# A decode layer of attention and MLP on one core: 64 KB rows in three slots, exp from PSUM, columns made on TensorE

## Chip, cores, metric

One core of one Trainium2 chip. The metric is the device time of one execution in microseconds (us), as the median of several runs. Each ratio compares a kernel with runs of the kernel before on the same chip.

## The reference, cut

One token, x of 1024 channels. The result is x + attention(LN x) + MLP-mixer(LN x). Attention reads a cache of 4 key heads of 65536 keys of 128 channels, each shared by 8 query heads:

```python
q = (xn @ wq)                                   # 1024 x 4096
scores = einsum("bhqd,bhkd->bhqk", q, k) * 128 ** -0.5
p = softmax(scores);  o = einsum("bhqk,bhkd->bhqd", p, v)
attn = o.reshape(B, 1, 4096) @ wo               # 4096 x 1024
# mixer: four groups of channels are shifted along the tokens, zeros move in
h = gelu(layernorm(x) @ w1);  hs = concat(shift(h, +1, -1, +2, -2)) @ w2
x1 = x + hs
out = x1 + gelu(layernorm(x1) @ w3) @ w4        # 1024 x 3584 x 1024
```

With one token, each shift leaves only zeros, so hs is zero whatever w1 and w2 are. K and V are 67.1 MB each, all weights together 35.7 MB: 169.87 MB in all.

## The kernel before

A list of loads is worked through in order. Loads go to five slots of 32 KB per partition (and one of 16 KB for w1, w2, wo); a load is issued as soon as its slot has been consumed. A unit is 16384 keys of one key head.

```python
BIG_BUFS = 5; UKEYS = 16384; SUBS = 2; SETS = 4
stream = [("wq",0), ("wq",1), ("w3",0), ("w3",1), ("w1",0), ("K",0), ("K",1), ("V",0)]
for u in range(2, NU):
    stream += [("K", u), ("V", u - 1)]            # K one unit ahead of V
    ...                                           # w2 and three wo in between
stream += [("wo", HKV - 1), ("V", NU - 1), ("w4", 0), ("w4", 1)]

def done(self, it):                               # called after the last reader of a tile
    self.tiles.pop(it); self.held[...] -= 1; self.pump()
...
            src = cache[0, g, b * UKEYS:(b + 1) * UKEYS, :].rearrange("(p ct) d -> p (ct d)", p=P)
            nc.sync.dma_start(out=t[:], in_=src)  # 128 rows of 32 KB
```

Keys lie in the rows with the channel inside, but the score products sum over partitions, so VectorE transposes K in place in blocks of 32 x 32 words. TensorE multiplies it with copies of the queries. Then the softmax of the unit and the product with V:

```python
    nc.vector.transpose(out=words, in_=words)                       # L372, 128 x 2048 words
    nc.tensor.matmul(sc[:, sub, :], lhsT=qdiag[:, c0:c0 + P], ...)  # L383, 32 per unit
    nc.vector.tensor_scalar(out=s_sb[:], in0=sc[:], scalar1=SCALE, ..., op1=ALU.max,
                            accum_out=mx[:])                        # L390, copy to SBUF with the maximum
    ...                                                             # maximum over partitions: L400 to L419
    nc.scalar.activation(out=p_sb[:], in_=s_sb, func=ACTF.Exp, bias=nball[:, b:b + 1], ...)   # L421
    nc.vector.transpose(out=pT, in_=p_sb)                           # L424
    nc.tensor.matmul(oacc[32 * q:32 * (q + 1), :], lhsT=pT[...], rhs=vt[...],
                     tile_position=(0, 32 * q))                     # L457, 32 per unit, four columns of tiles
```

A small clock of ticks spreads the softmax steps of unit u between the score products of unit u+1. At the end w4 comes in six pieces (8, 8, 8, 2, 1, 1 of its 28 columns), and its products wait for each piece. The h of the MLP goes to DRAM and back to become columns; x is loaded once as a row and once as 128 slivers of 16 bytes.

## Time and profile before

| | before |
|---|---|
| median | 405.87 us (405.79 to 405.95) |
| profiled span | 404.1 us |
| moved by the load queue | 169.87 MB in 6912 packets |
| DMA share and rate, 60 to 360 us | 1.00, 429 to 431 GB/s |
| busy PE, DVE, ACT | 58%, 52%, 8% |
| last 24 products of w4 | start at 397.63 us |

The DMA share is how much of the time the 16 DMA engines are busy on average. It is 1.00 over 300 us, so the DMA is the bound there. The packet count is worth a check against the code: the loads have 128 rows each, so 8 per DMA engine; 48 loads make 384 rows per engine, plus one completion per load and engine, 432, and 432 x 16 = 6912.

### The profile page before, as it was taken

The numbers are of one execution on the slowest core, as the hardware profiler recorded it, in microseconds if no ns is written. First come the engines' busy times: TensorE is split into PE (matmuls) and PEld (weight loads), VectorE is DVE, ScalarE is ACT, GpSimd is POOL, SyncE is SP. The second block draws the span as 40 slices with busy tenths as digits, with TensorE's granted clock in tenths as the row PEclk, the third lists the DMA queues.
The fourth block names the chain that finished last, engine by engine and source line by source line (L and its number), as shares of the span: only waits on it lengthen the run. The fifth ranks groups of instructions, "written<-read, shape, count | busy, mean of one in ns | idle before, by whom it ended". The sixth has DMA issues, their size and how long they took to land.

```text
span 404.1 us, 3287 instructions
## 1 busy us (share of the span) xinstructions
PE 236.2 (58%) x1392; PEld 94.1 (23%) x1392; DVE 211.8 (52%) x241; ACT 34.3 (8%) x61; POOL 6.4 (2%) x19
## 2 busy tenths in 40 slices
PE   0382727839483859292929394565658561948094
PEld 0131202313131323031313231122213220313041
DVE  0310046957658584566585473738393934665310
ACT  1000210110101011001010101010101010010100
POOL 4000100000000000000000000000000000000000
PEclk9998558688897979797978979596959895879769
DMA  8999999999999999999999999999999999999993
GB/s 357 422 415 431 449 416 439 440 418 429 448 417 425 454 409 430 444 431 417 448 428 418 436 420 438 428 444 423 428 436 428 422 436 435 431 426 430 420 427 144
DMA packets 7237, 170.11 MB, mean 421 GB/s; under 512 B 1070, under 2 KB 1074, under 8 KB 1462
## 3 DMA queue, kind: packets, MB, share of 16 engines
q1 hardware_dynamic: 6912, 169.87, 98.1%
q8 instruction: 11, 0.18, 0.2%
q0 software_dynamic: 160, 0.02, 0.0%
q10 hardware_dynamic: 150, 0.01, 0.0%
q14 instruction: 4, 0.03, 0.0%
HBM read 169.88 MB, written 0.01 MB: 420 GB/s over the span
## 4 chain that ended last, share of the span: by engine, by line
DMA 49%; PE 30%; DVE 10%; another core or an unknown queue 6%; ACT 2%; issue 2%; SPq 0%; DVEq 0%; ACTq 0%
DMA big<-in_A_k_cache_dram 35%; PE sc L383 21%; DMA big<-in_B_w_dram 11%; DVE big L372 5%; PE oacc L457 4%; DMA x_bf<-in_A_x_dram 3%; DVE s_sb L390 2%; PE psq L250 1%; ACT p_sb L421 1%; PE psB L179 1%; PE psB L239 1%; DVE pT L424 1%; PE pm_mx L400 1%; DVE og L439 0%
## 5 line engine op out<-in xcount | busy, mean ns | idle before, releaser
L383 PE MATMUL sc<-big,qdiag 128*128 128x512 bf16 x512 | 150.0, 461 | 104.9 <-DVE big L372 104.9
L372 DVE STREAM_TRANSPOSE big<-big 128x2048 f32<-128x2048 f32 x64 | 142.4, 2279 | 49.4 <-DMA big<-in_A_k_cache_dram 49.4
L383 PEld LDWEIGHTS <-qdiag 128*128 128x128 bf16 x512 | 56.8, 111 | 193.2 <-issue 100.3
L457 PE MATMUL oacc<-big,pT 128*32 128x512 bf16 x512 | 37.7, 396 | 9.7 <-DMA big<-in_A_v_cache_dram 9.7
L390 DVE TENSOR_SCALAR_CACHE_REDUCE s_sb<-sc 128x1024 f32<-128x1024 f32 x16 | 19.6, 1225 | 45.0 <-PE sc L383 45.0
L424 DVE STREAM_TRANSPOSE pT<-p_sb 128x1024 bf16<-128x1024 bf16 x16 | 19.8, 1240 | 16.8 <-ACT p_sb L421 16.8
L463 ACT COPY ob<-oacc 128x512 f32<-128x512 f32 x12 | 7.0, 586 | 214.6 <-PE oacc L457 214.6
L421 ACT ACTIVATE p_sb<-s_sb,nball 128x1024 bf16<-128x1024 f32 x16 | 18.4, 1150 | 76.5 <-DVE nball L419 76.5
L457 PEld LDWEIGHTS <-pT 128*32 128x32 bf16 x512 | 14.0, 99 | 28.7 <-issue 17.1
L400 PE MATMUL pm_mx<-ident_f,mx 128*1 128x128 f32 x16 | 4.3, 270 | 16.7 <-DVE s_sb L390 16.7
L419 DVE COPY nball<-pm_mx 128x1 f32<-128x1 f32 x16 | 2.5, 153 | 17.5 <-PE pm_mx L413 17.5
L250 PE MATMUL psh<-big,ln_rep_b 128*32 128x512 bf16 x56 | 5.5, 505 | 8.8 <-DMA big<-in_B_w_dram 8.8
L466 DVE SCALAR_TENSOR_TENSOR og<-oacc,wb,og 128x512 f32<-128x512 f32 x4 | 3.0, 751 | 12.5 <-PE oacc L457 12.5
L179 PE MATMUL psB<-big,cols_h 128*1 128x512 bf16 x56 | 7.7, 420 | 1.6 <-DMA big<-in_B_w_dram 1.6
L189 PE MATMUL pm_ln<-ln_rowsum_a,ones_f 128*128 128x1 f32 x2 | 0.6, 348 | 13.7 <-DVE sel L213 13.7
L179 PE MATMUL psB<-w,oT 128*1 128x512 bf16 x64 | 7.6, 379 | 0.0
L473 PE MATMUL pm_e<-og,selbig 128*128 128x128 f32 x32 | 5.6, 326 | 3.2 <-DVE nball L419 2.3
L402 DVE TENSOR_REDUCE negm<-pm_mx 1x8 f32<-1x128 f32 x16 | 4.4, 275 | 5.4 <-PE pm_mx L400 5.4
L250 PEld LDWEIGHTS <-ln_rep_b 128*32 128x32 bf16 x72 | 3.4, 120 | 15.0 <-issue 12.2
L183 DVE CAST xT<-x_bf 128x8 f32<-128x8 bf16 x1 | 0.2, 172 | 12.0 <-DMA x_bf<-in_A_x_dram 12.0
L400 PEld LDWEIGHTS pm_mx<-ident_f,mx 128*1 128x1 f32 x16 | 1.3, 79 | 21.9 <-DVE s_sb L390 21.9
L439 DVE SCALAR_TENSOR_TENSOR og<-ob,wb,og 128x512 f32<-128x512 f32 x8 | 6.0, 751 | 0.1
(98 smaller groups left out, 80.5 us busy)
## 6 DMA issues: line engine op xcount, KB each, us to landing
big<-in_A_k_cache_dram SPq DMA_DIRECT2D x16, 4096.0 KB, 46.1
big<-in_A_v_cache_dram SPq DMA_DIRECT2D x16, 4096.0 KB, 39.9
big<-in_A_wq_dram SPq DMA_DIRECT2D x2, 4096.0 KB, 16.9
w<-in_A_wo_dram SPq DMA_DIRECT2D x4, 2048.0 KB, 30.1
big<-in_B_w_dram SPq DMA_DIRECT2D x2, 3584.0 KB, 34.3
big<-in_B_w_dram SPq DMA_DIRECT2D x3, 2048.0 KB, 40.7
w<-in_B_w_dram SPq DMA_DIRECT2D x2, 2048.0 KB, 42.6
big<-in_B_w_dram SPq DMA_DIRECT2D x1, 512.0 KB, 43.4
```

Source lines behind the costliest of these rows:

```text
L179: nc.tensor.matmul(psB[32 * j:32 * j + 1, :], lhsT=lhsT, rhs=rhs, start=False, stop=False, tile_position=(0, 32 * j), skip_group_check=True)
L250: nc.tensor.matmul(acc[i][32 * q:32 * q + 32], lhsT=rep[:, c, :], rhs=wt[:, k, 512 * s:512 * (s + 1)], start=first, stop=last, tile_positi ...
L372: nc.vector.transpose(out=words, in_=words)
L383: nc.tensor.matmul(sc[:, sub, :], lhsT=qdiag[:, c0:c0 + P], rhs=cols[:, sub, s, :, b, :, r], start=(s == 0 and b == 0 and r == 0), stop=(s ...
L390: nc.vector.tensor_scalar(out=s_sb[:], in0=sc[:], scalar1=SCALE, scalar2=None, op0=ALU.mult, op1=ALU.max, accum_out=mx[:])
L400: nc.tensor.transpose(pm[0:1, 0:P], unit.pop((u, "mx"))[:, 0:1], ident_f[:])
L421: nc.scalar.activation(out=p_sb[:], in_=unit.pop((u, "ssb"))[:], func=ACTF.Exp, bias=nball[:, b:b + 1], scale=1.0, accum_out=group[(g, "la ...
L424: nc.vector.transpose(out=pT[:].rearrange("p u n -> p (u n)"), in_=p_sb[:].rearrange("p u n -> p (u n)"))
L439: nc.vector.scalar_tensor_tensor(out=og[:], in0=ob[:], scalar=wb[:, k:k + 1], in1=og[:], op0=ALU.mult, op1=ALU.add)
L457: nc.tensor.matmul(oacc[32 * q:32 * (q + 1), :], lhsT=pT[:, sub, 32 * t:32 * (t + 1)], rhs=vt[:, sub, :, t, :], start=(sub == 0 and t < 4) ...
L463: nc.scalar.copy(out=ob[:], in_=oacc[:])
L473: nc.tensor.matmul(pe[:, 0:P], lhsT=selbig[:, cg, :], rhs=og[:, 128 * cg:128 * (cg + 1)], start=(cg == 0), stop=(cg == 3))
```

## The change

Its intent: fewer and larger loads, fewer instructions, no trips through DRAM. Three parts:

1. All large loads go into three slots of 64 KB rows; a unit is 32768 keys, the score tile has four banks, and the pipelining by ticks goes.
2. The maximum and exp read the score tile in PSUM; the copy in SBUF goes.
3. x, h and the zero vector become columns by small TensorE products; w3 is read with a stride so that the columns come out in w4's order.

```diff
-UKEYS = 16384
-SUBS = 2
+ROW = 32768
+SUBS = 4
 SETS = 4
-BIG_BUFS = 5
-W4_PIECES = ((8, 8), (8, 2, 1, 1))
+SLOTS = 3
+W4_PIECES = (16, 8, 2, 1, 1)
 ...
+    stream = ["wq", "w3", "w12"]
+    for u in range(NU):
+        if u == NU - 1:
+            stream += [("K", u), "wo", ("V", u)]
+        else:
+            stream += [("K", u), ("V", u)]
+    stream.append("w4")
 ...
-    x_bf = const.tile([P, DC], BF16, name="x_bf")
-    nc.scalar.dma_start(out=x_bf[:], in_=A_x[0, 0, :].rearrange("(p c) -> p c", c=DC))
 ...
+    for c in range(DC):
+        nc.tensor.matmul(px[:, c:c + 1], lhsT=x_row[0:1, c::DC], rhs=pick4[0:1, 0:1], start=True, stop=True)
 ...
+        wt = st.tiles["w3"][:, 0:DC * F].rearrange("p (c m k) -> p c k m", c=DC, k=FC)
 ...
+        for ik in range(8):
+            nc.tensor.matmul(ph[:, ik, :], lhsT=h_rows[:, ik // 4, P * (ik % 4):P * (ik % 4 + 1)], rhs=pick4[:],
+                             start=True, stop=True)
 ...
-        s_sb = spool.tile([P, SUBS, 512], F32, name="s_sb", tag="s_sb")
-        nc.vector.tensor_scalar(out=s_sb[:], in0=sc[:], scalar1=SCALE, scalar2=None, op0=ALU.mult, op1=ALU.max,
-                                accum_out=mx[:])
+        nc.vector.reduce_max(out=mx[:], in_=sc[:].rearrange("p e n -> p (e n)"), axis=AX.X)
 ...
+        nc.scalar.activation(out=p_sb[:], in_=sc[:], func=ACTF.Exp, bias=nball[:, b:b + 1], scale=SCALE,
+                             accum_out=group["lall"][:, b:b + 1])
 ...
+    for u in range(NU - 1):
+        compute_k(u)
+        compute_v(u)
+    compute_k(NU - 1)
+    for g in range(HKV - 1):
+        project(g)
+    compute_v(NU - 1)
+    project(HKV - 1)
+    st.done("wo")
+    compute_w4(0, FC)
```

## The prediction

> **What bounds the kernel now.** I read the page first: slices, then the chain.
>
> ```profile
> span 404.1 us, 3287 instructions
> ...
> PE 236.2 (58%) x1392; PEld 94.1 (23%) x1392; DVE 211.8 (52%) x241; ACT 34.3 (8%) x61; POOL 6.4 (2%) x19
> ...
> DMA  8999999999999999999999999999999999999993
> ...
> q1 hardware_dynamic: 6912, 169.87, 98.1%
> ...
> DMA 49%; PE 30%; DVE 10%; another core or an unknown queue 6%; ACT 2%; issue 2%; SPq 0%; DVEq 0%; ACTq 0%
> ```
>
> The DMA row is full from the second slice to the last but one, while no engine passes 58%. The chain gives PE 30%, but that is the route the chain happened to take back through waits that cost nothing. Busy time by stretch settles it (columns: window, length, PE, PEld, DVE, ACT, POOL busy with counts, granted clock, DMA share, GB/s):
>
> ```profile
> 0.00:20.00 20.00, 3.19 (x8) 1.69 (x8) 4.29 (x30) 1.75 (x3) 4.76 (x16) 1.00 0.94 394
> ...
> 60.00:100.00 40.00, 30.25 (x130) 11.36 (x128) 28.33 (x24) 2.96 (x5) 0.00 (x0) 0.78 1.00 428
> ...
> 220.00:260.00 40.00, 21.71 (x147) 8.99 (x148) 20.32 (x24) 2.97 (x5) 0.00 (x0) 0.81 1.01 431
> ...
> 380.00:404.00 24.00, 15.08 (x114) 6.71 (x114) 1.69 (x5) 0.58 (x1) 0.00 (x0) 0.75 0.73 306
> ```
>
> PE and DVE work vary by a third between stretches; the DMA share stays at 1.00 and 428 to 431 GB/s. So the time is three terms: a start (394 against 430 GB/s over 20 us loses 36/430 x 20 = 1.7 us), 169.87 MB at 430 GB/s (395.0 us), and a tail. The last byte is then due near 396.7 us. The timeline of the end shows the tail:
>
> ```profile
> 383.05 3.61 PE L457 MATMUL oacc<-big,pT 128*32 128x512 bf16 x32 [9.68 <-DMA big<-in_A_v_cache_dram]
> ...
> 397.63 2.91 PE L179 MATMUL psB<-big,cols_h 128*1 128x512 bf16 x24 [1.55 <-DMA big<-in_B_w_dram]
> ...
> 400.58 0.58 ACT L526 CAST out_t<-psB 64x512 bf16<-64x512 f32 x1 [25.40 <-PE psB L179]
> ```
>
> The last 24 products start when pieces of w4 land, then cast and store: about 7 us after the last byte, of which the change can touch perhaps 3. The V tile before w4 has its last byte due at 396.7 - 7.34 MB/430 = 379.6 us, yet its matmuls start at 383.05: a load counts as landed some 3.4 us after its mean due time.
>
> **What the Trainium skill says.** "DMA: Bandwidth & Descriptors", section "Where 436 GB/s comes from", puts the ceiling of the 16 engines at 435.2 GB/s; the trace's 428 to 432 is 99% of it, so no arrangement of loads can win more than 1.2%. The same page, "Queues, rings and completion order", says a copy is split over up to 16 rings that complete apart, and nothing holds the faster ones back: that fits the 3.4 us of late landing without lost throughput. "SBUF — State Buffer", section "SBUF: two separate sides", says DMA and engine accesses don't contend; the stretches above agree. "TensorE: Matmul & The Clock Gate", Part 1, says the array runs at half clock until some 3.4 us of activity; the trace agrees (32 PV products take 3.61 us after the idle time above; 31 take 1.91 us when warm).
>
> **The change part by part.** Bytes: the same five weights, K and V; 169.87 MB stay, so 395.0 us stay unless the rate moves.
>
> Start: x's load in 128 slivers (12.4 us to landing in section 6 of the page) and the trips of h and the zero vector through DRAM go; one row and eight tiny matmuls come instead. The chain by which the first matmuls start at 22.7 us shortens by several us. But wq is now one 8.39 MB load, landing near 1.7 + 19.5 + 3.4 = 24.6 us, and meanwhile the DMA has wq, w3 and w12 (19.9 MB, until 48 us) queued. wq's 64 products took 5.5 us, so its slot is free for K 0 near 30 us, 18 us before the queue would run dry. Gain on the end: 0.
>
> A unit in the middle is now 16.8 MB, 2 x 19.5 = 39.0 us of DMA. Its compute, counted from K landing, from durations of before: four transposes of 4096 words, 2.27 us per 2048, so 4.5 us each, 18 us in all. 64 score products in four sets; 32 took 9.2 us before and 0.216 us each once warm, so a set of 16 (3.5 us) hides under the next transpose, and the last ends at 21.6 us: K's slot is free. Max over 2048 columns: twice the 1.23 us of the old pass over 1024, less the fixed part, 2.3. Two tiny transposes and three DVE steps, 1.3. Exp over 2048, from PSUM: twice 1.15, less the fixed part, plus its 0.19 read, 2.3. Transpose of P, 2.4. Sum 29.9. Then 64 PV products from a cooled array, 3.61 + 1.9 = 5.5, giving 35.4; every second unit a group epilogue of about 4, giving 39.4.
>
> Against the DMA's clock: V(u+1) goes into K(u)'s slot and is due to start at 39.0; the slot is free at 21.6, slack 17 us. K(u+2) goes into V(u)'s slot and is due at 58.5; free at 35.4, slack 23 us. The order listing of the changed kernel confirms that PE does K(u), then V(u) with nothing of K(u+1) between: the pipelining of the old kernel is gone and PE idles some 8 us per unit, but inside the DMA's time. Dropped DVE work (eight og passes of 0.75 us, fewer copies) is also beside the DMA. Sum of the middle: 0.
>
> Tail: the last V is now 8.39 MB, followed by w4. V lands near 383.0. Then PV 5.5 (388.5), og pass and hand-over 0.85 (389.4), row sums by five matmul calls 1.3 warm as near 223 us (390.7), four DVE steps 1.0 (391.7), projection of the last group, 16 products, 1.9 (393.6), w4's 56 products at 1.89/16 = 0.118 us, 6.6: 400.2 us. The pieces of w4 land before PE asks, save the last few near 399. Before, PE ended at 400.5. So the PE chain has become about as long as the DMA's: change -0.3 us. If rows of 64 KB make V land up to another row's time later (64 KB at 27 GB/s an engine, 2.4 us), it is +2.1; mean +0.9.
>
> Rate: 430 against 435.2 GB/s is 4.7 us over 6144 rows/16 engines = 384 rows, an estimate of 12 ns per row. Twice the row halves the count: up to -2.3 us. At the end, where rows are 16 KB, the trace had 426 GB/s, which points the same way but is within the scatter of short windows. I take -1.5.
>
> Sum: 405.87 + 0 + 0 + 0.9 - 1.5 = 405.3 us.
>
> **Rivals.** (1) Three slots starve the DMA. For: five slots gave finer release, and one 8 MB load can't start until a whole one is consumed. Against: the slacks of 17 and 23 us. It would take PE at half clock throughout: 64 scores at 0.427 = 27.3, chain 8.3, PV 7.2, epilogue 4, so 47 us per unit against 39, some 60 us slower. The trace has the clock rise within 4 us of each score burst, and the sets now follow each other with gaps of 1 us at most, so I hold this at 2%. (2) The tail is what grows: nothing of V 7 may start before 8.39 MB have landed, and the products of w4 queue behind it in PE's order. If V lands late and the array is cold again after the DVE steps (w4 at 0.213 us, +5.3), it is 409 to 413. (3) Large rows lift the rate to the ceiling, 433 GB/s: 403. (4) Large rows hurt: rows of one engine's neighbours lie twice as far apart in DRAM. Nothing in the trace speaks for it; 2% of rate would be +8 us.
>
> **Range and chances.** Rivals 2 and 3 span 402 to 411 with the body at 405; over 2% faster (below 397.8) would need 438 GB/s, above the ceiling, 2%; over 2% slower (above 414) needs rival 1 or 4, 5%; within 2%, 93%.
>
> **What would show it.** DMA share 1.00 in every middle stretch, at 430 to 433 GB/s; DVE transposes near 4.5 us; PE idle before V for P's chain, and DVE idle before each K for the load; K's loads issued over 10 us before the queue is dry; the last PV starting at 382 to 386 us, PE ending at 399 to 403. Wrong would be: any middle stretch with a DMA share below 0.97 (slots), a rate under 425 at full share (rows), or w4's products beginning later than 397 us (tail).

## The result, and the profile after

404.15 us median (404.00 to 404.71) against 405.90 in the same rounds. The recorded ratio of the fast runs is 0.9945, with a 95% interval of 0.9919 to 0.9972; the four runs of each kernel that the record lists give 0.996 by their means as by their medians, so the recorded ratio must rest on further runs, and I go by the medians. That is the same within 2%, though 1.75 us, and it lies in the predicted range.

The page of the changed kernel (engine line: busy us, share, instructions; DMA line: busy tenths in 40 slices; queue line: packets, MB, share; then the chain that ended last):

```profile
span 402.3 us, 3130 instructions
...
PE 231.5 (58%) x1392; PEld 91.0 (23%) x1392; DVE 197.1 (49%) x141; ACT 26.9 (7%) x35; POOL 5.5 (1%) x29
...
DMA  9989999999999999999999999999999998999993
...
q1 hardware_dynamic: 4128, 169.87, 98.0%
...
DMA 51%; DVE 18%; PE 14%; ACT 2%; issue 0%; SPq 0%; DVEq 0%; ACTq 0%
```

DVE lost 15 us of work and ACT 7, and the time did not follow. The queue moved the same 169.87 MB in 4128 packets instead of 6912: 232 rows per DMA engine instead of 384 (8 per load, but 32 for wo, which is now one load of four rows per partition), and 26 loads instead of 48 (258 x 16 = 4128). Longer stretches than the prediction's show the rate, because those of 40 us scatter more in this kernel (423 to 443 GB/s, before 428 to 432). Busy time by stretch, before:

```profile
60.00:140.00 80.00, 54.91 (x287) 21.15 (x289) 55.87 (x53) 6.60 (x12) 0.00 (x0) 0.82 1.00 429
140.00:220.00 80.00, 49.38 (x273) 19.65 (x265) 50.70 (x48) 6.60 (x12) 0.00 (x0) 0.83 1.00 429
220.00:300.00 80.00, 45.98 (x279) 18.33 (x280) 46.33 (x50) 6.60 (x12) 0.00 (x0) 0.81 1.00 431
```

and after (same columns):

```profile
60.00:140.00 80.00, 44.56 (x236) 17.32 (x236) 45.96 (x22) 6.75 (x8) 0.81 (x4) 0.76 1.00 433
140.00:220.00 80.00, 49.27 (x322) 20.20 (x318) 47.54 (x27) 4.88 (x6) 0.81 (x4) 0.81 1.00 433
220.00:300.00 80.00, 48.25 (x287) 19.78 (x280) 48.39 (x28) 4.88 (x6) 0.81 (x4) 0.77 1.01 435
```

The share is 1.00 in both; the rate is up from about 430 to about 433 GB/s. One unit of the changed kernel, from its timeline (start, us, engine, line, operation; in brackets the idle time before and what ended it):

```profile
147.60 17.42 DVE L296 STREAM_TRANSPOSE big<-big 128x4096 f32<-128x4096 f32 x4
152.14 16.56 PE L301 MATMUL sc<-big,qdiag 128*128 128x512 bf16 x64 [5.46 <-DVE big L296]
168.73 0.33 SPq L118 DMA_DIRECT2D big<-in_A_v_cache_dram  x1
168.74 2.29 DVE L306 TENSOR_REDUCE mx<-sc 128x1 f32<-128x2048 f32 x1 [3.72 <-PE sc L301]
...
174.58 2.31 DVE L322 STREAM_TRANSPOSE p_sb<-p_sb 128x2048 bf16<-128x2048 bf16 x1 [2.18 <-ACT p_sb L319]
176.94 5.53 PE L351 MATMUL oacc<-big,p_sb 128*32 128x512 bf16 x64 [4.75 <-DVE p_sb L322]
182.52 0.33 SPq L118 DMA_DIRECT2D big<-in_A_k_cache_dram  x1
...
186.26 17.42 DVE L296 STREAM_TRANSPOSE big<-big 128x4096 f32<-128x4096 f32 x4 [9.37 <-DMA big<-in_A_k_cache_dram]
```

K's slot is free after 21.1 us (147.60 to 168.73, where the next load is issued), V's after 34.9 us, and the next K lands after 38.7 us, for which VectorE had to wait 9.37 us. (This unit's transposes follow a group's epilogue and don't wait themselves; K lands every 38.7 us, 108.88 to 186.26 us for two.) So each unit waits for the load, with the softmax in plain sight between the two products, and nothing is lost. The tail after:

```profile
381.55 5.62 PE L351 MATMUL oacc<-big,p_sb 128*32 128x512 bf16 x64 [9.10 <-DMA big<-in_A_v_cache_dram]
...
390.37 1.89 PE L151 MATMUL psB<-big,oT 128*1 128x512 bf16 x16 [1.07 <-DVE oT L380]
...
392.10 3.62 PE L151 MATMUL psB<-big,hT 128*1 128x512 bf16 x32
396.07 2.90 PE L151 MATMUL psB<-big,hT 128*1 128x512 bf16 x24 [0.35 <-DMA big<-in_B_w_dram]
```

Again the last 24 products wait for pieces of w4 and take 2.9 us, as before the change; they start at 396.07 instead of 397.63 us. Of the 1.8 us between the two profiled spans, 1.56 are there when the last pieces land; the rest, some 0.2 us, comes after the final store is issued (2.91 us from there to the end before, 2.68 after).

### The profile page after: what moved, and what is told of

The parts are those of the page before. It is cut to its first block, busy times and chain, and to the rows that moved or that the text cites. A ratio compares the mean times of both kernels' runs of the same rounds, so it can differ in the third digit from the quotient of the medians.

```text
span 402.3 us, 3130 instructions
## 1 busy us (share of the span) xinstructions
PE 231.5 (58%) x1392; PEld 91.0 (23%) x1392; DVE 197.1 (49%) x141; ACT 26.9 (7%) x35; POOL 5.5 (1%) x29
## 3 DMA queue, kind: packets, MB, share of 16 engines
q1 hardware_dynamic: 4128, 169.87, 98.0%
HBM read 169.87 MB, written 0.00 MB: 422 GB/s over the span
## 4 chain that ended last, share of the span: by engine, by line
DMA 51%; DVE 18%; PE 14%; ACT 2%; issue 0%; SPq 0%; DVEq 0%; ACTq 0%
DMA big<-in_A_k_cache_dram 43%; DVE big L296 14%; DMA big<-in_B_w_dram 8%; PE sc L301 7%; PE oacc L351 4%; DVE p_sb L322 2%; DVE mx L306 2%; ACT p_sb L319 2%; PE psB L151 1%; PE ps L272 1%; DVE m L310 0%; PE pm_mx L308 0%; PE pm_mx L315 0%; DVE rep L312 0%; ACT out_t L409 0%
## 5 line engine op out<-in xcount | busy, mean ns | idle before, releaser
L301 PE MATMUL sc<-big,qdiag 128*128 128x512 bf16 x512 | 131.3, 419 | 65.0 <-DVE big L296 64.9
L296 DVE STREAM_TRANSPOSE big<-big 128x4096 f32<-128x4096 f32 x32 | 139.4, 4413 | 51.3 <-DMA big<-in_A_k_cache_dram 51.3
L351 PE MATMUL oacc<-big,p_sb 128*32 128x512 bf16 x512 | 44.4, 522 | 43.6 <-DVE p_sb L322 34.5
L306 DVE TENSOR_REDUCE mx<-sc 128x1 f32<-128x2048 f32 x8 | 18.3, 2291 | 30.5 <-PE sc L301 30.5
L351 PEld LDWEIGHTS <-p_sb 128*32 128x32 bf16 x512 | 16.8, 126 | 68.3 <-DVE p_sb L322 35.1
L319 ACT ACTIVATE p_sb<-sc,nball 128x2048 bf16<-128x2048 f32 x8 | 15.7, 1967 | 221.6 <-DVE nball L317 221.6
L322 DVE STREAM_TRANSPOSE p_sb<-p_sb 128x2048 bf16<-128x2048 bf16 x8 | 18.5, 2311 | 18.0 <-ACT p_sb L319 18.0
L218 PE MATMUL psh<-big,ln_rep_b 128*32 128x512 bf16 x56 | 14.2, 1050 | 10.2 <-DMA big<-in_B_w_dram 10.2
L151 PE MATMUL psB<-big,oT 128*1 128x512 bf16 x64 | 7.2, 379 | 1.1 <-DVE oT L380 1.1
L151 PE MATMUL psB<-big,hT 128*1 128x512 bf16 x56 | 6.5, 379 | 0.4 <-DMA big<-in_B_w_dram 0.4
## 6 DMA issues: line engine op xcount, KB each, us to landing
big<-in_B_w_dram SPq DMA_DIRECT2D x3, 2048.0 KB, 40.3
```

Source lines behind the costliest of these rows:

```text
L151: nc.tensor.matmul(psB[32 * j:32 * j + 1, :], lhsT=lhsT, rhs=rhs, start=False, stop=False, tile_position=(0, 32 * j), skip_group_check=True)
L218: nc.tensor.matmul(acc[32 * q:32 * q + 32, i, :], lhsT=rep[:, c, :], rhs=cols(c, 2 * q + i), start=(c == 0), stop=(c == DC - 1), tile_posi ...
L301: nc.tensor.matmul(sc[:, e, :], lhsT=qdiag[:, c0:c0 + P], rhs=cols[:, s, e, :, b2, :, r], start=(s == 0 and b2 == 0 and r == 0), stop=(s = ...
L306: nc.vector.reduce_max(out=mx[:], in_=sc[:].rearrange("p e n -> p (e n)"), axis=AX.X)
L319: nc.scalar.activation(out=p_sb[:], in_=sc[:], func=ACTF.Exp, bias=nball[:, b:b + 1], scale=SCALE, accum_out=group["lall"][:, b:b + 1])
L322: nc.vector.transpose(out=flat, in_=flat)
```

## The experiments

Theory R (rows): each row costs a DMA engine a fixed time beside its bytes, so fewer rows end the stream earlier. Rivals: the small transfers that part 3 removes; the lighter compute (part 2 and the rest); and, for the tail, that PE's chain and not the landing sets the end. Ten kernels ran.

| run | rows per DMA engine | median us | ratio to before (95%) |
|---|---|---|---|
| before | 384 | 405.90 | |
| changed | 232 | 404.15 | 0.9945 (0.9919 to 0.9972) |
| half_rows | 376 | 405.47 | 0.9988 (0.9976 to 0.9999) |
| eighth_rows | 1240 | 413.40 | 1.0182 (1.0169 to 1.0195) |
| eighth_one_load | 1128 | 412.55 | 1.0149 (1.0126 to 1.0172) |
| before_cols | 384 | 406.94 | 1.0023 (1.0005 to 1.0040) |
| before_psumexp | 384 | 406.69 | 1.0017 (1.0001 to 1.0034) |
| psumexp_warm | 384 | 405.85 | 0.9990 (0.9977 to 1.0003) |
| two_slots | 232 | 459.31 | 1.1301 (1.1271 to 1.1331) |
| no_w12 | 216 | 394.64 | 0.9708 (0.9686 to 0.9730) |
| w4_fine | 240 | 404.16 | 0.9942 (0.9922 to 0.9962) |
| best | 224 | 394.81 | 0.9719 (0.9705 to 0.9734) |

**half_rows and eighth_rows.** The changed kernel with its row-contiguous loads cut along the row:

```diff
+            def cut(out, in_):
+                w = out.shape[-1] // PARTS          # PARTS = 2 or 8
+                for j in range(PARTS):
+                    go(out[:, w * j:w * (j + 1)], in_[:, w * j:w * (j + 1)])
 ...
-                go(out=t[:], in_=cache[...])
+                cut(out=t[:], in_=cache[...])
```

> The changed kernel with wq, w3 and every K and V load cut into two loads of half rows (32 KB), in the same three slots. Row theory: the last pieces of w4 landed 1.56 us earlier in the changed kernel (396.07 against 397.63 us) because it has 258 instead of 432 packets per DMA engine (4128 and 6912 over 16), so 9 ns per packet, an estimate; 18 loads cut in two give 18 x 9 = 162 packets more per engine, so +1.5 us: 405.6 us. Rival (the small transfers that went, or the lighter compute, made the gain): unchanged, 404.2 us within 0.4.

> The same with eight loads of an eighth of the row (8 KB) each. Row theory: 18 x 7 x 9 = 1134 packets more per engine, at 9 ns +10 us: 414 us. Rival: 404 us, or less, since each transpose could start before the whole tile has landed, which matters only if compute bounds.

Measured 405.47 and 413.40 us, as R had it. Both still run at full DMA share; the rate goes down, to 430 or 431 GB/s in half_rows. Stretches of eighth_rows:

```profile
60.00:140.00 80.00, 47.60 (x270) 19.49 (x270) 47.25 (x28) 6.17 (x7) 0.81 (x4) 0.79 1.01 421
140.00:220.00 80.00, 46.69 (x270) 19.59 (x270) 48.98 (x28) 4.88 (x6) 0.81 (x4) 0.78 1.01 421
```

**eighth_one_load.** These two raised rows and loads together. To part them, each K and V load stays one load, but reads eight stretches of 8 KB per partition. Keys are permuted in the same way in K and V, which leaves the result as it is.

```diff
-                go(out=t[:], in_=cache[...].rearrange("(p ct) d -> p (ct d)", p=P))
+                go(out=t[:].rearrange("p (h n) -> p h n", h=8),
+                   in_=cache[...].rearrange("(h p ct) d -> p h (ct d)", h=8, p=P))
```

> The changed kernel with each K and V load still one load, but made of eight rows of 8 KB per partition (the same permutation of the keys in K and V, to which the result is blind). It adds 16 x 8 x 7 = 896 rows per DMA engine and no load. If the cost found with half and eighth rows (8.1 and 8.2 ns per packet) belongs to the row: +7.3 us, 411.5 us. If it belongs to the load (its completion, its issue): no change, 404.2 us.

The load queue shows the rows, 1128 and 26 loads per engine (1154 x 16):

```profile
q1 hardware_dynamic: 18464, 169.87, 98.9%
```

Measured 412.55 us: 8.40 us for 896 rows, 9.4 ns each. The cost is the row's. Charging all of the other two runs to rows gives 1.32/144 = 9.2 and 9.25/1008 = 9.2 ns; their 18 and 126 more loads cost nothing that shows. Nor does the order of addresses: eighth_rows reads its 8 KB at steps of 64 KB, eighth_one_load at steps of 8 KB. The middle alone, without start and tail, agrees: K lands every 38.70 us in the changed kernel (108.88 to 302.38 us, five units) and every 39.73 us in eighth_one_load (110.38 to 309.01 us), which is 1.03 us for 112 rows, 9.2 ns.

**before_cols and before_psumexp.** Parts 3 and 2 alone, put into the kernel before. In the second:

```diff
-        nc.vector.tensor_scalar(out=s_sb[:], in0=sc[:], scalar1=SCALE, ..., op1=ALU.max, accum_out=mx[:])
-        unit[(u, "ssb")] = s_sb
+        nc.vector.reduce_max(out=mx[:], in_=sc[:].rearrange("p e n -> p (e n)"), axis=AX.X)
+        unit[(u, "ssb")] = sc
```

(with the scale moved into the maximum and exp); the first takes over the small products, the strided read of w3 and the plain zero vector from the changed kernel.

> The kernel before with only the third part of the change: x, h and the zero vector made into columns without a trip through DRAM and without the load of x in 128 slivers. Small-transfer theory: it gets the gain, 404.2 us. Row theory: 20 packets per engine fewer, -0.2 us: 405.7 us. Both expect the first matmuls of w3 to take longer, as in the changed kernel (14.2 us there), with no effect on the end.

> The kernel before with only the second part of the change: maximum and exp straight from the score tile in PSUM, no copy in SBUF. Row theory and small-transfer theory: 405.9 us, no change. Rival that the lighter compute made the gain: 404 to 405 us.

Neither has the gain; both medians are a little above the kernel before. The single runs of before_psumexp tell more: 405.87, 405.95, 406.01, then 407.37, 407.44, 407.51, two heaps with nothing between. The profiled run was of the upper heap. The last 24 products there:

```profile
397.81 4.42 PE L179 MATMUL psB<-big,cols_h 128*1 128x512 bf16 x24 [3.04 <-DMA big<-in_B_w_dram]
```

They landed 0.18 us later than before the change (397.63), yet took 4.42 instead of 2.91 us. The granted clock, third number from the end, was 0.50 from 398 to 400 us there and 1.00 in the kernel before (second line):

```profile
398.00:400.00 2.00, 2.00 (x12) 0.63 (x10) 0.00 (x0) 0.00 (x0) 0.00 (x0) 0.50 0.19 69
398.00:400.00 2.00, 2.00 (x22) 0.79 (x17) 0.00 (x0) 0.00 (x0) 0.00 (x0) 1.00 0.18 68
```

PE had idled 3.04 us instead of 1.55 us for that piece.

**psumexp_warm.** The kernel of before_psumexp with 20 products of constants into a spare PSUM tile, meant for PE's idle time ahead of the last pieces:

```diff
+    pw = ps_O.tile([P, 512], F32, name="oacc")
+    for k in range(20):
+        nc.tensor.matmul(pw[32 * (k % 2):32 * (k % 2) + 1, :], lhsT=vals["hT"][:, 0:1], rhs=qdiag[:, 0:512], ...)
     compute_w4(1)
```

> The kernel before with exp from PSUM, and 20 products into a scratch tile in the wait before the last piece of w4. Without them the runs fell in two heaps, 405.9 and 407.4 us, and in the profiled run of the upper heap the last 24 products took 4.42 us after 3.04 us of idle PE, against 2.91 us after 1.55 us in the kernel before. If a cooled array is the upper heap: one heap at 405.9 us, last products 2.9 us. If it is chance elsewhere: two heaps again.

```profile
397.76 2.87 PE L179 MATMUL psB<-big,cols_h 128*1 128x512 bf16 x24 [1.91 <-DMA big<-in_B_w_dram]
```

One heap, 405.71 to 405.98 us in six runs. The 20 products did not go where I meant them: the profile has them in three groups between 386.5 and 394.1 us, where they held up the 16 products before the last ones (393.75 us instead of 392.88). So PE idled 1.91 us instead of 3.04 before the last 24, and these stayed at 2.87 us. That fits the upper heap being a cooled array (a PE that runs at the lower clock after idling) in the last 3 us; part 2 alone is then worth nothing and costs nothing within 0.1 us (405.85 against 405.95 us). A few runs of the kernel before, at 407.0 to 408.1 us, look like the same; none of them has a profile. They widen the intervals of the table. For before_cols the same long idle, 3.10 us, and slow last products, 4.05 us, stand in its profile; its runs spread from 405.37 to 407.88, and I did not run it warm, so what part 3 alone is worth stays open; its fastest run is 0.4 us under the fastest of the kernel before.

**two_slots.**

```diff
-SLOTS = 3
+SLOTS = 2
```

> The changed kernel with two slots instead of three. By the slacks: K(u+1) can then be issued only when K(u)'s slot is free, 21.1 us after K(u) has landed (342.58 to 363.71 us in the changed kernel), while the load of V(u) ends 2.7 us short of 19.5 us after that landing; some 5.8 us of empty queue per unit for six units, 8 us at the start (K 0 waits for w3's slow products), and about 20 us at the end (w4 is issued only when the last V has been consumed). Sum 63 us: 467 us, DMA share near 0.85 in the middle. If slots did not matter at all, as compute is off the path: 404 us.

Measured 459.31 us. Here the rival mechanism of the prediction is made real. Timeline of one unit, and one stretch:

```profile
163.33 17.42 DVE L296 STREAM_TRANSPOSE big<-big 128x4096 f32<-128x4096 f32 x4 [5.34 <-DMA big<-in_A_k_cache_dram]
...
184.83 0.33 SPq L118 DMA_DIRECT2D big<-in_A_k_cache_dram  x1
...
206.58 17.42 DVE L296 STREAM_TRANSPOSE big<-big 128x4096 f32<-128x4096 f32 x4 [13.55 <-DMA big<-in_A_k_cache_dram]
```

```profile
140.00:220.00 80.00, 40.60 (x243) 16.43 (x242) 43.64 (x27) 4.88 (x6) 0.81 (x4) 0.70 0.93 394
```

The next K is issued when K's slot is free, 21.50 us after landing, and lands 21.75 us later: 43.25 us for this unit (43.6 on average over six, 42.9 to 44.4) against 38.7. The share falls to 0.93. I had expected 44.8 us per unit, a share of 0.85 and 467 us in all, 8 us too many. Likely I charged a load in an empty queue with both a start and the full late landing of a load in a full one; no run shows that.

**no_w12.**

```diff
-    stream = ["wq", "w3", "w12"]
+    stream = ["wq", "w3"]
 ...
-    compute_w12()
```

> The changed kernel without loading and multiplying w1 and w2: with one token the shifts fill every channel with zeros, so their product is zero and the result the same. 4.19 MB less, at 433 GB/s 9.7 us less: 394.5 us if the time is bytes by rate plus a fixed start and tail. If something else than the stream of loads bound the middle (units of compute, the slots), the first K would come 9.7 us earlier with the same effect, so this run tells only whether the whole stream moves; a gain under 8 us would speak against the sum of three terms.

Measured 394.64 us: 9.51 us less than the changed kernel for 4.19 MB (9.7 at 433 GB/s). Bytes come off the time at the rate of the stream. The result stays correct, for this shape only: with two or more tokens w1 and w2 matter.

**w4_fine.**

```diff
-W4_PIECES = (16, 8, 2, 1, 1)
+W4_PIECES = (16, 4, 4, 2, 1, 1)
```

> The changed kernel with the piece of 8 columns of w4 cut into 4 and 4. If the end is set by the landing of that piece (its 24 last products start at 396.07, after a wait of 0.35 us, and take 2.9 us), products start sooner and only those of the last pieces stay behind the landing: 0.5 to 1.0 us less, 403.4 us. If PE's chain after the last V sets the end, as my prediction had it: no change, 404.2 us.

Measured 404.16 us, no change, and the profile shows why the gain I hoped for isn't there:

```profile
391.89 6.51 PE L151 MATMUL psB<-big,hT 128*1 128x512 bf16 x54
398.65 0.38 PE L151 MATMUL psB<-big,hT 128*1 128x512 bf16 x2 [0.25 <-DMA big<-in_B_w_dram]
```

Now 54 products run through without a wait, and the last two wait 0.25 us for the last piece. PE's chain and the last landing end within a third of a microsecond of each other, so moving one alone gives nothing.

**best.** Both of the last two edits.

> The changed kernel without w1 and w2 and with the finer pieces of w4: the sum of what the two give alone, 393.8 us if the pieces give 0.7 us; 394.5 us if they give nothing.

Measured 394.81 us, the pieces again giving nothing. So the simpler no_w12 does as well, at 394.64 us, 2.8% under the kernel before by the medians.

## Why the prediction was right

**The bound.** Right: full share in every middle stretch of all versions with three slots, and bytes taken out come off the time at the stream's rate (no_w12). One of my alarms rang: two stretches of 40 us showed 423 GB/s, under the 425 I had named, at a share of 0.98. The first (100 to 140 us) was scatter: its neighbours have 443 and 438, and over 80 us it is 433. The second (300 to 340 us) is not made up beside it (436 and 431): the last K landed 40.2 us after the one before (302.38 to 342.58 us) instead of 38.7. half_rows has the same step (40.3 us), no_w12 one load later, and the kernel before loses about as much between 275 and 339 us, by an estimate from its landings (422 instead of 431 GB/s). So some 1.5 us go there in all of them, whatever the rows; the cause is open.

**Rows.** Right in mechanism, and the size came out close with some luck: the prediction estimated 12 ns per row from the distance to the ceiling, thought the count would halve, and took 1.5 us without working it out. The count fell by 152, not 192, for which 12 ns would be 1.8 us. The experiments give 9.2 to 9.4 ns, so 1.4 us of the measured 1.75. The other 0.35 us is not assigned for sure, but it points to part 3. In the profiles, the three kernels that keep the trips through DRAM end 2.82 to 2.91 us after the final store is issued, the nine without them 2.62 to 2.75 us; in before_cols this is 0.24 us less than in the kernel before, and its last pieces land 0.10 us earlier, which alone would be within the scatter.

**Slots.** Right that three suffice, and the unit was sized well: K's slot was told free after 21.6 us and V's after 35.4 (21.1 and 34.9 measured). The slack was told as 17 us; it is some 3 us less, because the queue runs dry at the last byte and not at the landing some 3 us later, from which I had counted. two_slots shows what the other side of that margin looks like.

**Start.** Right that nothing comes of it. The first products did not start several us sooner, though: those of wq began at 22.67 us (before 22.68), as soon as wq had landed, which was 2 us earlier than the 24.6 told. And one cost was overlooked: w3's products with the strided read. They took 5.5 us before (contiguous, in two halves)

```profile
31.30 1.91 PE L250 MATMUL psh<-big,ln_rep_b 128*32 128x512 bf16 x28 [0.85 <-DMA big<-in_B_w_dram]
...
41.15 3.61 PE L250 MATMUL psh<-big,ln_rep_b 128*32 128x512 bf16 x28 [7.93 <-DMA big<-in_B_w_dram]
```

and 14.2 us after:

```profile
40.97 14.16 PE L218 MATMUL psh<-big,ln_rep_b 128*32 128x512 bf16 x56 [10.24 <-DMA big<-in_B_w_dram]
```

as well as in before_cols, which keeps the loads in halves:

```profile
32.55 7.18 PE L251 MATMUL psh<-big,ln_rep_b 128*32 128x512 bf16 x28 [4.16 <-DMA big<-in_B_w_dram]
...
40.90 7.18 PE L251 MATMUL psh<-big,ln_rep_b 128*32 128x512 bf16 x28 [1.18 <-DMA big<-in_B_w_dram]
```

So the read makes the difference, and it is larger than 5.5 to 14.2 says: the granted clock was 1.00 in both halves of before_cols, but 0.50 in the second half of the kernel before. At full clock, 28 products took 1.91 us contiguous and 7.18 us strided. In the changed kernel it was paid from slack: V 0 was issued at 55.16 us and due behind K 0 near 67 us (an estimate: 28.3 MB at 433 GB/s and the start).

**Tail.** This term was mis-sized. I had put +0.9 us, as the mean of no change and a V tile that lands later by another 64 KB row. Measured: 0. The final products start at the landing and take 2.9 us in both kernels. V's matmuls started at 381.55 us, 1.50 us earlier than before; the 144 rows fewer ahead of V are worth 1.3 us of that at 9.3 ns. So the longer row did not make the landing later. (In the middle, K landed some 3.1 us behind a queue that starts at 1.7 us and moves 433.5 GB/s, an estimate.) The chain itself was right: 17.2 us from V's start to PE's end predicted, 17.4 measured; with the earlier V, its start and its end (398.97 us) both fell just below the times foretold.

The sum said 405.3 us and the measurement was 404.15; 0.9 of the difference is the tail term. The stated range ended at 411 us, although rival 2 had been sized at 409 to 413.

## What to carry to other kernels

Here, with a DMA share of 1.00 nearly from end to end, removed instructions, removed copies and removed overlap were worth nothing that these runs could measure; what moved the time was bytes, the cost per row and the few microseconds at both ends, and each could be sized from the trace beforehand. Where a trace shows such a share, these are the terms to look at first. Before pipelining is thrown away for larger tiles, the check is one of slots: when the slot comes free against when the queue runs dry; here three slots leave some 14 us and two lose over 4 us per unit. And a product chain at the very end should not wait long enough to cool: after 3 us of idle PE the last products took 1.5 us longer here, after 1.6 or 1.9 us they did not.

## What the Trainium skill lacked or had wrong

- "DMA: Bandwidth & Descriptors" (sections "Measured" and "Why small descriptors are slow") gives a rule for the size of a load, some 10.5 ns per packet for a load of 4 KB, and an overhead per packet for descriptors of 256 bytes; nothing for rows of many KB. Here, in a full queue, loads of 1 MB and 8 MB with the same 8 KB rows cost the same, and what counts is the row: 9.2 to 9.4 ns per row and DMA engine, from 8 to 64 KB; 421, 430 and 433 GB/s with rows of 8, 32 and 64 KB.
- No page says how late a load lands behind its mean due time in a full queue: some 3 us here by the estimates above, no longer for rows of 64 KB than of 32 KB, which is what slots have to be planned with.
- "SBUF — State Buffer", on its 16-byte lines, says that a read that crosses to a new line with every element pays a penalty, without a size for TensorE: w3 read with a step of 28 bf16 took 7.18 us for 28 products against 1.91 us contiguous, both at a granted clock of 1.00.
